# Attention with chunk selection, then an MLP: loads of later batches held behind W2, pair 4 prepared later, some ScalarE work on VectorE, the last rows in two parts

## The chip, the cores and the metric

The kernel runs on one core of one Trainium2 chip. A core has TensorE (matrix products), VectorE, ScalarE, GpSimd and SyncE, each with its own instruction queue that it works off in order, and 16 DMA engines that all queues share. The metric is the device time of one execution in microseconds (us). The time is the median of several runs; the profile is of one execution of its own.

## The reference

There are 4 batches, 8 heads, 768 positions, 64 numbers per head. Keys come in 24 chunks of 32 positions. For each query an upper bound of its scores in each chunk decides which six chunks it may look at. Then come masked attention over these, a layer norm, and an MLP with a residual.

```python
def _attn_ref(q, k, v):
    k_min, k_max = min and max of k over each chunk of 32
    ub = sum over d of maximum(q * k_min, q * k_max)
    ub = where(causal, ub, -1e9)
    top_chunks = argsort(ub)[..., -6:]
    scores = scale * q @ k.T
    scores = where(chunk selected and pos_q >= pos_k, scores, -1e9)
    return softmax(scores) @ v

def _moe_ref(x, g_ln, w_ch1, w_ch2):
    xn = (x - mean(x)) / sqrt(var(x) + 1e-6) * g_ln
    return x + maximum(xn @ w_ch1, 0.0) @ w_ch2
```

x has the 8 heads of a position side by side (512 numbers). W1 is 512 x 2048, W2 is 2048 x 512, all in float32 outside; the kernel works with float16 for the large products.

## The kernel before

**Tiling.** Two heads form a pair, so that 2 x 64 numbers fill 128 partitions. There are 16 pairs, g = 0 to 15, four for each batch; batch 0 has pairs 0 to 3, and pair 4 is the first of batch 1. The 768 positions are six tiles of 128, in two halves (r or i = 0, 1) of three tiles each.

**A pair.** `load_qk` (L190) loads a half of q and k in four transfers on SyncE's queue into tiles of a pool with six buffers per name. `turn` (L219) transposes them on TensorE into PSUM. `q_copy` and `k_copy` bring them to float16: in batch 0 straight into the operands QA, QB, KA, KB on ScalarE; in later batches into `qh` and `kh`, from which SyncE copies them by DMA into QA, QB (`q_ring`) and KA, KB. `k_bound` (VectorE) takes the min and max of each chunk, `k_diag` lays them out (GpSimd for later batches: four small operations), `bounds` (TensorE) forms the upper bounds, `select` (VectorE) finds the six best, `mask_t` and `mask_ring` put the mask into QA and QB as further rows. `scores` are TensorE products followed by an exponential on ScalarE; `diag` (GpSimd) cuts the diagonal; `values` are the products with v, `normalise` and `pair_stats` (VectorE) finish a pair.

**A half of a batch.** When four pairs are done: `stats`, `centre`, `x_t` (transposes on TensorE), `mlp1` (8 groups of 8 matmuls with W1, each group followed by a ReLU on ScalarE, L516), `mlp2` (for each of three tiles 16 matmuls with W2 in four pieces, j = 0 to 3, then on VectorE the scaling and the residual, L530, and the output transfer on SyncE, L535).

**Order.** TensorE is given work of several pairs and of the MLP interleaved. Each call is a piece with a time in units of one pair; the pieces are sorted by it, and the engines work them off in that order. For batch 0 a list (`begin`, with `loads` for the transfers) gives the order and each engine is tied to it; for later pairs `at(t, ...)` gives times relative to T, the time of the pair's first score. `MOVED` holds some 400 small shifts of single pieces.

**Weights.** W1 and W2 are loaded by GpSimd's queue in four pieces each, converted to float16 on the way (`w1_load`, `w2_load`). A one-element copy from `kc`, which some pair's `k_bound` wrote, holds each load back until that pair is so far. V loads go through the same queue. A transfer of GpSimd takes one of eight completion semaphores in turn and waits for the transfer that had it before.

The warm-up matmuls (`warm`, `idle`, L309) write to tiles that nobody reads.

Of the kernel before, what the change touches and what calls it, by code (L numbers as in the profile page):

```python
# [9 lines left out]
ACTF = mybir.ActivationFunctionType  # L10
ALU = mybir.AluOpType
# [8 lines left out]
def kernel(  # L20
# [13 lines left out]
    nc = tc.nc  # L34
# [52 lines left out]
    RT = const.tile([P, S], F16, name="RT", tag="RT")  # L87
    tiny = const.tile([1, 1], F32, name="tiny", tag="tiny")
# [75 lines left out]
    def w2_load(j, g):  # L164
        nc.gpsimd.tensor_copy(w2b[0:1, 4 * j, 0:1], st[g]["kc"][0:1, 0, NCH // 2:NCH // 2 + 1])
        nc.gpsimd.dma_start(w2b[:, 4 * j:4 * j + 4, :], w2_r[:, 4 * j:4 * j + 4, :])

# [22 lines left out]
    def load_qk(g, i):  # L190
        b, hp = divmod(g, HP)
        for nm, src in (("kn", k), ("qn", q)):
            t = st[g][nm, i] = ldp.tile([P, TR, 2, D], F32, name=nm, tag=nm)
            for hh in range(2):
                nc.sync.dma_start(
                    t[:, :, hh], src[b, 2 * hp + hh, i * TR * P:(i + 1) * TR * P].rearrange("(t p) d -> p t d", p=P),
                )

# [72 lines left out]
    def k_copy(g, i):  # L271
        pst = st[g]["kn", i]
        c = cols(g, i)
        if g < HP:
            nc.scalar.copy(KA[g % NK][0:64, c], pst[0:64, :])
            nc.scalar.copy(KB[g % NK][64:P, c], pst[64:P, :])
            return
        kh = smp.tile([P, TR * P], F16, name="kh", tag="kh")
        nc.scalar.copy(kh, pst)  # L279
        nc.sync.dma_start(KA[g % NK][0:64, c], kh[0:64, :])  # L280
        nc.sync.dma_start(KB[g % NK][64:P, c], kh[64:P, :])
# [223 lines left out]
    def mlp1(b, r, m):  # L505
# [10 lines left out]
        nc.scalar.activation(h["hT"][:, m:m + 2], hp_[:, :, 0:TR * P], ACTF.Relu, scale=HS)  # L516

    def mlp2(b, r, i, j):
# [4 lines left out]
        for kt in range(4 * j, 4 * j + 4):  # L523
            nc.tensor.matmul(  # L524
                yp, h["hT"][:, kt, i * P:(i + 1) * P], w2b[:, kt, :],
                start=(kt == 0), stop=(kt == KT2 - 1),
            )
        if j == 3:
            ot = outp.tile([P, DM], F32, name="ot", tag="ot")
            nc.vector.scalar_tensor_tensor(  # L530
                ot, yp, h["rstd"][:, i:i + 1], xh(b, r)[:, i].rearrange("p h d -> p (h d)"),
# [3 lines left out]
            nc.sync.dma_start(out[b, s * P:(s + 1) * P, :], ot)  # L535
# [11 lines left out]
        4: [(load_v, 1, 1), (load_v, 2, 1), (load_qk, 4, 0)],  # L547
        5: [(w2_load, 0, 0), (w2_load, 1, 0), (load_v, 3, 1), (load_qk, 4, 1)],
        6: [(w2_load, 2, 1), (w2_load, 3, 1)],
# [65 lines left out]
    GAP = 0.6  # L615
# [7 lines left out]
    floor = {tuple(args): t for t, _, fn, args, _ in pieces if fn == load_qk}  # L623
    ready = [max(t for t, _, fn, args, _ in pieces if fn == x_t and args[1] == r) + 0.01 for r in range(NR)]
    for g in range(HP, NG):
# [5 lines left out]
        for i in range(2):  # L631
            t = max(T - 1.98 + 0.3 * i, floor.get((g, i), -1.5) + 0.01)
# [5 lines left out]
        at(T - 1.4, q_relu, g)  # L638
        at(T - 1.4, q_ring, g)
        at(T - 1.3, k_diag, g)  # L640
# [21 lines left out]
    for b in range(B):  # L662
# [14 lines left out]
        if b == 0:  # L677
# [13 lines left out]
            (): -0.04, (0, 1): -0.009, (0, 2): -0.025, (1,): 0.008, (1, 1): 0.017, (1, 2): 0.017,  # L691
            (2,): 0, (2, 4): 0.006, (2, 5): 0.028, (3,): 0, (3, 1): 0.013, (3, 2): 0.013,
            (4,): -0.048, (5,): 0.008, (5, 5): 0.016, (6,): 0.004, (7,): -0.067, (7, 1): -0.07,
            (8,): -0.436, (9,): -0.025, (9, 5): -0.02, (11,): -0.044, (12,): -0.311, (13,): -0.144,
            (14,): -0.138, (14, 5): -0.134, (15,): -0.21, (15, 4): -0.176, (15, 5): 0,
        },
        "centre": {
            (): 0.008, (0,): -0.017, (0, 1): 0, (0, 1, 0): -0.017, (1,): 0, (1, 0, 2): 0.089,
            (1, 1): 0.033, (1, 1, 1): 0.026,
        },  # L700
        "diag": {
            (): -0.046, (0, 0): 0.016, (0, 1): 0.001, (1, 0): 0.012, (1, 1): -0.067, (2,): 0.003,
            (3, 0): -0.003, (3, 1): 0, (4,): -0.056, (6, 0): -0.044, (6, 1): -0.066, (7, 0): -0.178,
            (7, 1): -0.097, (8, 0): -0.399, (8, 1): -0.6, (9, 0): -0.066, (9, 1): -0.069, (11, 0): 0,
            (11, 1): -0.054, (12, 0): -0.04, (12, 1): 0, (13, 0): -0.146, (13, 1): -0.078,
            (14, 0): 0.003, (14, 1): 0, (15, 0): -0.621,
        },
        "k_bound": {
            (0,): -0.011, (1,): -0.011, (2,): -0.009, (3,): -0.018, (4, 0): 0.007, (4, 1): 0.027,
            (5, 1): 0.022, (6, 0): 0.002, (6, 1): 0.107, (7,): -0.058, (8, 0): -0.331,  # L710
            (8, 1): -0.396, (9, 0): 0.002, (9, 1): 0.065, (11, 0): -0.008, (11, 1): 0.025,
            (12, 0): -0.017, (12, 1): -0.015, (13,): -0.032, (14,): 0.028,
        },
        "k_copy": {
            (0,): -0.004, (1, 0): 0.161, (1, 1): 0.063, (2,): 0.006, (3, 0): -0.011, (3, 1): 0.054,
            (4,): 0.024, (5, 0): 0.511, (5, 1): 0.42, (6,): 0.038, (7, 0): -0.032, (9, 1): 0.023,
            (10,): 0.034, (11, 1): 0.026, (12, 0): 0.938, (12, 1): 0.253, (13, 0): 0.002,
            (13, 1): 0.073, (14,): 0.046, (15,): 0.034,
        },
        "k_diag": {  # L720
            (1,): 0.041, (2, 0): 0.13, (3, 0): 0.033, (3, 1): 0.01, (4,): -0.002, (6,): 0.002,
            (7,): -0.058, (8,): -0.331, (9,): -0.138, (10,): -0.023, (11,): 0.02, (12,): 0.006,
            (13,): -0.032, (14,): -0.108, (15,): -0.076,
        },
        "load_qk": {
            (): -0.438, (0, 0): 0.085, (0, 1): -0.538, (1, 0): 0.034, (1, 1): -0.331, (2, 0): 0,
            (2, 1): -0.329, (3, 0): 0.16, (3, 1): -0.169, (4, 0): -0.33, (4, 1): -0.667,
            (5, 0): -0.543, (5, 1): -1.259, (6, 0): 0.011, (6, 1): -0.111, (7, 0): 0.064,
            (7, 1): 0.002, (8, 0): -0.299, (8, 1): -0.593, (10, 0): 0.015, (10, 1): -0.002,
            (11, 0): -0.01, (11, 1): -0.012, (12, 0): 0.082, (12, 1): 0.004, (13, 0): 0.11,  # L730
            (13, 1): 0.159, (14,): 0.026, (15, 0): 0.317, (15, 1): 0.334,
        },
        "load_v": {
            (2,): -0.087, (3, 0): -0.13, (3, 1): -0.568, (4,): -0.551, (5,): -0.547, (6,): -0.163,
            (7,): 0.215, (8,): -0.124, (9,): 0.342, (12,): 0.279, (13,): 0.241, (14,): 0.301,
            (15,): 0.238,
        },
        "mask_ring": {
            (): 0.017, (0, 0): 0.021, (0, 1): 0, (1, 0): 0.036, (1, 1): -0.009, (2, 0): 0.023,
            (2, 1): 0, (4,): 0.064, (5,): 0.074, (6,): 0.076, (7,): 0.016, (8,): -0.257, (9,): 0.076,  # L740
            (10,): 0.209, (11,): 0.066, (12,): 0.08, (13,): 0.102, (14,): 0.139, (15,): 0.093,
        },
        "mask_t": {
            (): -0.004, (0,): 0, (1, 0): -0.019, (1, 1): -0.002, (2,): 0.002, (4,): -0.016,
            (5,): -0.068, (7,): -0.064, (8,): -0.337, (10,): -0.001, (11,): -0.014, (12,): 0.002,
            (13,): -0.082, (14,): 0, (15,): -0.006,
        },
        "mlp1": {
            (0, 0, 2): -0.016, (0, 0, 6): 0.106, (0, 0, 10): 0.098, (0, 0, 14): 0.069,
            (0, 1): -0.023, (0, 1, 0): 0, (0, 1, 2): 0.016, (0, 1, 14): 0.055, (1,): -0.026,  # L750
            (1, 0, 0): 0.016, (1, 0, 2): 0.016, (1, 0, 4): 0.028, (1, 0, 8): -0.014,
            (1, 1, 0): -0.036, (1, 1, 4): -0.178, (1, 1, 10): 0, (1, 1, 14): -0.001, (2,): -0.294,
            (2, 0, 6): -0.616, (2, 0, 12): -0.277, (2, 1, 2): -0.353, (2, 1, 6): -0.28,
            (2, 1, 10): -0.228, (3,): 0.103, (3, 0, 2): 0, (3, 0, 4): 0, (3, 0, 12): 0,
            (3, 0, 14): 0, (3, 1, 0): 0, (3, 1, 4): 0.108, (3, 1, 6): 0, (3, 1, 14): 0.094,
        },
        "mlp2": {
            (): -0.156, (0, 0, 1, 0): -0.071, (0, 0, 1, 3): 0, (0, 0, 2, 0): -0.051, (0, 1): -0.154,
            (0, 1, 0): -0.156, (0, 1, 0, 0): -0.184, (0, 1, 0, 3): -0.145, (0, 1, 1, 0): -0.156,
            (0, 1, 1, 1): 0.152, (0, 1, 2, 0): -0.132, (1,): -0.157, (1, 0, 0, 1): 0,  # L760
            (1, 0, 1, 3): -0.053, (1, 1): -0.138, (1, 1, 0): -0.182, (1, 1, 0, 3): -0.138,
            (1, 1, 2, 2): -0.182, (1, 1, 2, 3): -0.182, (2,): -0.298, (2, 0, 0): -0.323,
            (2, 0, 0, 1): -0.46, (2, 0, 0, 3): -0.305, (2, 0, 1, 0): -0.323, (2, 0, 2, 2): -0.34,
            (2, 0, 2, 3): -0.34, (2, 1): 0, (2, 1, 0, 0): -0.34, (2, 1, 0, 1): -0.18,
            (2, 1, 0, 2): -0.323, (2, 1, 0, 3): -0.298, (2, 1, 1, 0): -0.267, (2, 1, 1, 1): -0.298,
            (2, 1, 1, 2): -0.423, (2, 1, 1, 3): -0.568, (3,): -0.233, (3, 0, 0): 0,
            (3, 0, 0, 2): -0.124, (3, 0, 0, 3): -0.233, (3, 0, 2): -0.332, (3, 1, 0, 0): -0.332,
            (3, 1, 0, 1): -0.374, (3, 1, 1, 1): -0.263, (3, 1, 1, 2): -0.443, (3, 1, 1, 3): -0.009,
# [122 lines left out]
```

## Time and profile before

| what | value |
|---|---|
| time, median of 3 runs | 303.1 us (302.56 to 303.96) |
| span of the profiled execution | 301.4 us, TensorE clock 0.997 |
| TensorE busy | 288.2 us (96%) |
| VectorE, ScalarE, GpSimd busy | 190.8, 183.5, 91.1 us |
| DMA traffic | 27.27 MB read from HBM, 6.29 MB written |
| W1 pieces, issue to landing | 6.0, 7.3, 8.2, 10.6 us |
| W2 pieces, issue to landing | 8.1, 10.1, 12.3, 14.3 us |
| mean of one: L524 (mlp2), L512 (mlp1) matmul | 379 ns, 326 ns |
| mean of one: L516 ReLU, L276 K copy on ScalarE | 813 ns, about 470 ns |

The page says PE for TensorE, DVE for VectorE, ACT for ScalarE, POOL for GpSimd, SP for SyncE; a q behind it means that engine's instruction queue. L512 is line 512 of the kernel. Matmuls overlap one another, so that the mean of one is longer than the distance between two, and a TensorE shown as busy may still be working below its best rate.

### The profile page before, as it was taken

The page shows a single profiled execution, that of the slowest core. Times are in us where ns is not written, and L with a number is a line of the kernel's source. Part 1 is how long each engine was busy: PE and PEld are TensorE (multiplying, and loading weights), DVE is VectorE, ACT ScalarE, POOL GpSimd, SP SyncE. Part 2 cuts the span into 40 slices and gives each one's busy share as a digit, 9 for nine tenths or more (in the row PEclk, how much of TensorE's full clock was granted, in tenths as well). Part 3 has the DMA queues.
Part 4 walks back from the last instruction along what each step waited for, and adds up shares of the span by engine and source line. Part 5 has one row for each costly group of instructions (what it writes and reads, how often), then busy time and mean ns, then how long its engine had stood idle before and what let it go on. Part 6 is the DMA issues. An engine that isn't in the chain of part 4 may idle for free.

```text
span 301.4 us, 7194 instructions
## 1 busy us (share of the span) xinstructions
PE 288.2 (96%) x2753; PEld 195.4 (65%) x2753; DVE 190.8 (63%) x654; ACT 183.5 (61%) x274; POOL 91.1 (30%) x162
## 2 busy tenths in 40 slices
PE   7887998999999999999999999999999999999993
PEld 3874766765777676777767667766666555555541
DVE  7888655679998788999577768577262282011011
ACT  3983997664788667778665674848368524423310
POOL 9559383152444412733230411223021120000000
PEclk9999999999999999999999999999999999999998
DMA  7999999999659649679572210113010110010111
GB/s 131 208 210 198 180 199 196 164 193 204 149 135 187 124 72 165 110 143 148 88 132 62 78 46 2 41 49 90 35 37 0 37 37 35 35 37 35 70 37 71
DMA packets 90226, 31.41 MB, mean 104 GB/s; under 512 B 78416, under 2 KB 87120, under 8 KB 90192
## 3 DMA queue, kind: packets, MB, share of 16 engines
q1 hardware_dynamic: 60416, 23.61, 33.8%
q0 software_dynamic: 29248, 7.34, 24.8%
q8 instruction: 22, 0.36, 0.5%
q14 instruction: 12, 0.10, 0.1%
q10 hardware_dynamic: 528, 0.00, 0.1%
HBM read 27.27 MB, written 6.29 MB: 111 GB/s over the span
## 4 chain that ended last, share of the span: by engine, by line
PE 75%; DMA 8%; POOL 7%; issue 4%; DVE 4%; ACT 1%; POOLq 0%; ACTq 0%
PE yp L524 24%; PE mm L512 24%; PE mm L411 10%; PE sm L437 6%; PE tr L223 4%; DMA w2b<-in_moe_w_ch_dram 4%; DMA w1b<-in_moe_w_ch_dram 4%; PE ub L326 3%; POOL va L214 2%; PE trh L497 1%; POOL pt L424 1%; PE trh L354 1%; DVE xc L482 1%; ACT pt L417 1%; POOL rstd L491 1%
## 5 line engine op out<-in xcount | busy, mean ns | idle before, releaser
L417 ACT ACTIVATE pt<-mm 128x1024 f16<-128x1024 f32 (+1 forms) x96 | 86.2, 918 | 25.7 <-PE mm L411 25.3
L524 PE MATMUL yp<-w2b,hT 128*128 128x512 f16 x384 | 95.9, 379 | 1.5 <-DMA w2b<-in_moe_w_ch_dram 1.5
L512 PE MATMUL mm<-xT,w1b 128*128 128x384 f16 x512 | 94.3, 326 | 0.0
L516 ACT ACTIVATE hT<-mm 128x768 f16<-128x768 f32 x64 | 51.9, 813 | 49.1 <-PE mm L512 48.8
L512 PEld LDWEIGHTS <-w1b 128*128 128x128 f16 x512 | 48.9, 98 | 29.9 <-issue 0.2
L524 PEld LDWEIGHTS <-hT 128*128 128x128 f16 x384 | 36.4, 98 | 31.8
L424 POOL TENSOR_SCALAR_AFFINE_SELECT pt<-pt 128x768 f16<-128x768 f16 x32 | 28.8, 899 | 89.1 <-ACT pt L417 89.1
L530 DVE SCALAR_TENSOR_TENSOR ot<-yp,rstd,x 128x512 f32<-128x512 f32 x24 | 17.9, 746 | 45.9 <-PE yp L524 45.9
L411 PE MATMUL mm<-QA,KA 128*128 128x128 f16 (+2 forms) x224 | 34.5, 245 | 1.0 <-ACT hT L516 0.5
L411 PE MATMUL mm<-QB,KB 128*128 128x128 f16 (+2 forms) x224 | 34.2, 246 | 0.0
L437 PEld LDWEIGHTS <-pt 128*128 128x128 f16 x672 | 24.6, 98 | 5.6 <-POOL pt L424 1.8
L437 PE MATMUL sm<-va,pt 128*128 128x65 f16 x672 | 26.5, 193 | 1.4 <-POOL pt L424 1.3
L411 PEld LDWEIGHTS <-KA 128*128 128x128 f16 x224 | 17.9, 99 | 8.1 <-issue 2.3
L471 DVE BATCH_NORM_STATS2 bst<-x 128x6 f32<-128x128 f32 x96 | 21.9, 282 | 0.8
L268 DVE TENSOR_REDUCE kc<-tr 128x12 f32<-128x384 f32 x32 | 17.6, 549 | 6.6 <-PE tr L223 4.9
L411 PEld LDWEIGHTS <-KB 128*128 128x128 f16 x224 | 18.0, 98 | 3.5 <-issue 0.8
L446 DVE RECIPROCAL rden<-sm 128x6 f32<-128x6 f32 x32 | 6.1, 191 | 19.7 <-PE sm L437 19.6
L447 DVE TENSOR_TENSOR x<-sm,rden 128x384 f32<-128x384 f32 x32 | 17.8, 557 | 1.0
L223 PE MATMUL tr<-ident_f,qn 128*128 128x128 f32 x96 | 16.2, 278 | 1.3 <-DMA qn<-in_q_dram 1.3
L269 DVE TENSOR_REDUCE kc<-tr 128x12 f32<-128x384 f32 x32 | 17.5, 547 | 0.0
L279 ACT CAST kh<-tr 128x384 f16<-128x384 f32 x24 | 11.6, 484 | 9.2 <-DMA KB<-kh 3.2
L223 PE MATMUL tr<-ident_f,kn 128*128 128x128 f32 x96 | 16.2, 278 | 0.0
(87 smaller groups left out, 354.2 us busy)
## 6 DMA issues: line engine op xcount, KB each, us to landing
kn<-in_k_dram SPq DMA_DIRECT2D x64, 96.0 KB, 3.3
qn<-in_q_dram SPq DMA_DIRECT2D x64, 96.0 KB, 3.7
out_dram<-ot SPq DMA_DIRECT2D x24, 256.0 KB, 2.1
va<-in_v_dram POOLq DMA_DIRECT2D x12, 192.0 KB, 5.5
w1b<-in_moe_w_ch_dram POOLq DMA_DIRECT2D x4, 512.0 KB, 7.7
w2b<-in_moe_w_ch_dram POOLq DMA_DIRECT2D x4, 512.0 KB, 11.2
KA<-kh SPq DMA_DIRECT2D x24, 48.0 KB, 2.1
KB<-kh SPq DMA_DIRECT2D x24, 48.0 KB, 2.0
```

Of the source, the lines that this page charges most:

```text
L223: nc.tensor.transpose(pst[:, t * P:(t + 1) * P], src[:, t], ident_f)
L268: nc.vector.tensor_reduce(kc[:, 0, n], view, axis=AX.X, op=ALU.min)
L411: nc.tensor.matmul(sc[:, hh, o:o + w * P], ks[:, t * P:(t + 1) * P], qs[:, s * P:(s + w) * P], start=True, stop=True,)
L417: nc.scalar.activation(pt[:, n0:n1].rearrange("p n h x -> p h n x"), sc[:, :, 0:o].rearrange("p h (n x) -> p h n x", x=P), ACTF.Exp, scale ...
L424: nc.gpsimd.affine_select(out=dv, in_=dv, compare_op=ALU.is_ge, fill=0.0, base=0, pattern=[[0, 2 * TR], [1, P]], channel_multiplier=-1,)
L437: nc.tensor.matmul(pv[:, hh, s2, :], pt[:, where[t, s], hh, :], va[:, hh, t, 0:D + 1], start=(t == 0), stop=(t == s),)
L447: nc.vector.tensor_tensor(xh(b, r)[:, :, 2 * hp:2 * hp + 2, :].rearrange("p s h d -> p h s d"), pv[:, :, :, 0:D], rden.to_broadcast([P, 2, ...
L471: nc.vector.bn_stats(h["st"][:, i, hp], xh(b, r)[:, i, 2 * hp:2 * hp + 2].rearrange("p h d -> p (h d)"),)
L512: nc.tensor.matmul(hp_[:, i, 0:TR * P], w1b[:, kt, (m + i) * P:(m + i + 1) * P], h["xT"][:, kt], start=(kt == 0), stop=(kt == KT1 - 1),)
L516: nc.scalar.activation(h["hT"][:, m:m + 2], hp_[:, :, 0:TR * P], ACTF.Relu, scale=HS)
L524: nc.tensor.matmul(yp, h["hT"][:, kt, i * P:(i + 1) * P], w2b[:, kt, :], start=(kt == 0), stop=(kt == KT2 - 1),)
L530: nc.vector.scalar_tensor_tensor(ot, yp, h["rstd"][:, i:i + 1], xh(b, r)[:, i].rearrange("p h d -> p (h d)"), op0=ALU.mult, op1=ALU.add,)
```

## The change

**q/k loads held.** Before the first load of pair 4, SyncE issues a tiny transfer (`fence`) that reads one element of W2's last piece, so it has to wait until that piece is there; all later q/k loads are ordered after it. Meant: W1 and W2 have the DMA engines to themselves. **W2 earlier in the list.** W2's pieces wait for pair 3's `kc`, go out in pairs, and V's second halves are spread between the weights; pair 4's loads move from list entries 4 and 5 to 6. **Pair 4 later.** Its transposes and copies get the time -1.0 (`LATE`), where before they followed their load. **ScalarE's work on VectorE.** In the first MLP half (b, r) = (0, 0), every second ReLU (m = 2, 6, 10, 14) is a `tensor_scalar` on VectorE; in batch 0 the second-half copy into KB is too. **The last tile** of the last half is computed in two column parts, 384 and then 128 columns, with eight of the 16 row blocks per call, and each part is scaled and written out by itself. **MOVED** is redone throughout.

```diff
     def w2_load(j, g):
-        nc.gpsimd.tensor_copy(w2b[0:1, 4 * j, 0:1], st[g]["kc"][0:1, 0, NCH // 2:NCH // 2 + 1])
+        nc.gpsimd.tensor_copy(w2b[0:1, 4 * j, 0:1], st[g]["kc"][0:1, 0, 0:1])
...
     def load_qk(g, i):
         b, hp = divmod(g, HP)
+        done = nc.cur_bb.bb.instructions
+        if (g, i) == (HP, 0):
+            nc.sync.dma_start(fence, w2b[0:1, KT2 - 1, 0:1])
+            held.append(done[-1].name)
+        n = len(done)
...
+        if held:
+            for one in done[n:]:
+                if one.engine == nc.sync.engine:
+                    tc.add_manual_dep(one, held[0], order, reason="order")
...
-            nc.scalar.copy(KB[g % NK][64:P, c], pst[64:P, :])
+            (nc.scalar.copy if i == 0 else nc.vector.tensor_copy)(KB[g % NK][64:P, c], pst[64:P, :])
...
-        nc.scalar.activation(h["hT"][:, m:m + 2], hp_[:, :, 0:TR * P], ACTF.Relu, scale=HS)
+        if (b, r) == (0, 0) and m % 4 == 2:
+            nc.vector.tensor_scalar(
+                h["hT"][:, m:m + 2], hp_[:, :, 0:TR * P], 0.0, HS, op0=ALU.max, op1=ALU.mult,
+            )
+        else:
+            nc.scalar.activation(h["hT"][:, m:m + 2], hp_[:, :, 0:TR * P], ACTF.Relu, scale=HS)
...
-        for kt in range(4 * j, 4 * j + 4):
+
+        n, cs = 4, slice(0, DM)
+        if (b, r, i) == (B - 1, NR - 1, TR - 1):
+            n, cs = 8, slice(0, DM - P) if j < 2 else slice(DM - P, DM)
+        for kt in range(n * j % KT2, n * j % KT2 + n):
             nc.tensor.matmul(
-                yp, h["hT"][:, kt, i * P:(i + 1) * P], w2b[:, kt, :],
+                yp[:, cs], h["hT"][:, kt, i * P:(i + 1) * P], w2b[:, kt, cs],
                 start=(kt == 0), stop=(kt == KT2 - 1),
             )
-        if j == 3:
+        if kt == KT2 - 1:
...
-        4: [(load_v, 1, 1), (load_v, 2, 1), (load_qk, 4, 0)],
-        5: [(w2_load, 0, 0), (w2_load, 1, 0), (load_v, 3, 1), (load_qk, 4, 1)],
-        6: [(w2_load, 2, 1), (w2_load, 3, 1)],
+        4: [(load_v, 1, 1), (w2_load, 0, 3), (w2_load, 1, 3)],
+        5: [(load_v, 2, 1), (w2_load, 2, 3), (w2_load, 3, 3), (load_v, 3, 1)],
+        6: [(load_qk, 4, 0), (load_qk, 4, 1)],
...
-    GAP = 0.6
+    GAP, LATE = 0.6, -1.0
...
-            t = max(T - 1.98 + 0.3 * i, floor.get((g, i), -1.5) + 0.01)
+            t = max(T - 1.98 + 0.3 * i, LATE + 0.25 * i if g == HP else -9.0)
...
-        at(T - 1.4, q_relu, g)
-        at(T - 1.4, q_ring, g)
-        at(T - 1.3, k_diag, g)
+        t = max(T - 1.4, t + 0.1)
+        at(t, q_relu, g)
+        at(t, q_ring, g)
+        at(t + 0.1, k_diag, g)
```

## The prediction, made before the changed kernel ran

> **What bounds the kernel now.** I read the page's busy shares and slices first, then the table of windows, then TensorE's timeline, then the landing times of single transfers. The page:
>
> ```profile
> PE 288.2 (96%) x2753; PEld 195.4 (65%) x2753; DVE 190.8 (63%) x654; ACT 183.5 (61%) x274; POOL 91.1 (30%) x162
> ...
> PE   7887998999999999999999999999999999999993
> ...
> DMA  7999999999659649679572210113010110010111
> ```
>
> TensorE is the bound, but not evenly: apart from the last slice only the first seven (to 53 us) fall below 9, and there the DMA engines are full (they stay so to about 75 us). The table of windows (columns: busy us and count of PE, PEld, DVE, ACT, POOL; clock; DMA share; GB/s) shows who sets the pace there:
>
> ```profile
> 20.00:24.00 4.00, 2.55 (x49) 2.03 (x50) 3.26 (x13) 2.53 (x4) 2.74 (x5) 1.00 1.23 228
> ...
> 32.00:36.00 4.00, 4.00 (x34) 3.22 (x33) 2.34 (x11) 3.93 (x9) 0.76 (x1) 1.00 1.41 173
> 36.00:40.00 4.00, 3.66 (x28) 2.65 (x26) 2.01 (x11) 3.94 (x8) 3.36 (x6) 1.00 1.69 182
> 40.00:44.00 4.00, 3.60 (x33) 2.67 (x33) 2.07 (x5) 4.00 (x7) 3.41 (x8) 1.00 1.26 205
> 44.00:48.00 4.00, 4.00 (x40) 3.38 (x39) 2.67 (x5) 3.93 (x9) 1.61 (x3) 1.00 1.24 200
> 48.00:52.00 4.00, 3.42 (x47) 2.27 (x44) 2.70 (x13) 3.21 (x5) 2.02 (x3) 1.00 1.20 192
> 52.00:56.00 4.00, 3.04 (x25) 2.26 (x25) 2.40 (x7) 1.85 (x3) 0.00 (x0) 1.00 1.39 177
> ```
>
> From 29 to 49 us ScalarE has no idle time while VectorE is little over half busy: TensorE is paced by ScalarE's evictions. Busy TensorE hides this, so I count its work: a W1 matmul costs 0.1625 us in a dense run (8 in 1.30), a W2 matmul 0.216 (4 in 0.86), a 128x128 one 0.055, an f32 transpose 0.107. From mlp1's start at 28.4 to mlp2's first matmul at 49.5 the queue holds 17.5 us of such work: 3.6 us are lost. From 80 us on some 1 us in 10 is lost, so 28 to 53 is where something can be won. Then W2 itself is late:
>
> ```profile
> 49.53 1.89 PE L524 MATMUL yp<-w2b,hT 128*128 128x512 f16 x8
> 52.96 0.38 PE L524 MATMUL yp<-w2b,hT 128*128 128x512 f16 x1 [1.54 <-DMA w2b<-in_moe_w_ch_dram]
> ```
>
> The reason stands in GpSimd's timeline: two V loads wait for W1 pieces to land, and W2's issue stands behind them.
>
> ```profile
> 32.34 0.76 POOL L214 DMA_DIRECT2D va<-in_v_dram  x1 [1.82 <-DMA w1b<-in_moe_w_ch_dram]
> 36.02 0.77 POOL L214 DMA_DIRECT2D va<-in_v_dram  x1 [2.93 <-DMA w1b<-in_moe_w_ch_dram]
> ```
>
> W2's four pieces are issued at 38.15 to 41.88 and land 8.1, 10.1, 12.3 and 14.3 us later (46.3 to 56.2). SyncE is meanwhile loading q/k of batch 1 (its first load issues at 19.5).
>
> **What the Trainium skill says.** DMA: Bandwidth & Descriptors, section Issuing engines are not separate DMA queues: transfers from all engines interleave on the same 16 DMA engines. The trace agrees: a kn load lands in 4.2 to 6.0 us at 14 to 18 us, and in 13.8 to 14.1 when issued at 42 to 46 among W2. VectorE: DVE Perf Modes, section Why PSUM operands drop a tier: an fp32 operand in PSUM is read one element a cycle; here 384 such elements take 0.549 us (the k reduce) and 512 take 0.746 (the output eviction). PSUM — Partial Sum Buffer, section PSUM bank collisions raise a hardware error: a bank must not be touched by two engines at once, even in different columns, so it has to be guarded as a whole; no run here shows a collision.
>
> **The change part by part.**
>
> *ScalarE's relief.* Four ReLUs leave ScalarE (0.70 us each in its dense run, 2.8) and four K copies (0.48, 1.9); pair 4's two q/k evictions that stand at 47.7 and 48.8 (0.39 + 0.5) move past the stretch. Of 20.2 us of dense ScalarE work from 29.1, 15.3 remain, ending near 44.5.
>
> *VectorE's load.* It takes four ReLUs of 128x768 from PSUM. No row shows this; I extend 384 → 0.549 and 512 → 0.746: at least 0.80 (768 at 0.96 GHz, page above), at most 1.1; I take 0.87. The copies take about 0.4: 5.1 us in all. Summing the changed program's VectorE queue from the first xT copy (28.1) to the masks before mlp2 gives 17.1 us: it fits, ending near 46, but with hardly any slack.
>
> *TensorE.* Its total work is unchanged (the same matmuls, the same fillers). From 28.2 the changed order holds 16.7 us before mlp2's first matmul; with about 1 us in 10 lost (buffer rotation behind the four exponentials of pair 0), it gets there at 46.3 instead of 49.5.
>
> *W2 earlier.* In the new GpSimd order two W2 pieces go out right after rstd (0,0), with no landing to wait for; only the second two follow a V load that waits for W1's last piece. From 24 us no q/k loads compete. A W piece alone: they follow each other at 3.3 to 3.4 us (49.55, 52.92, 56.2) with some q/k beside, at 4.8 to 5.2 with q/k in full flow (22.1, 27.3, 32.1); a V or q/k transfer takes some 0.4 us of the engines. Taking off the q/k share leaves 2.3 to 2.9 per piece. W1 then lands at 22, 25, 30.5, 33; W2 at 36, 39, 43 and 45.4 to 48. mlp2's ninth matmul needs the third piece at about 48: no wait, and 1.5 us come free. At that matmul the changed kernel leads by 53.0 - 48.0 = 5.0 us.
>
> *The fence, a new wait.* SyncE waits for W2's last piece (call it F, 45.4 to 48, I take 46.7). Behind it on SyncE stand 28 q/k transfers of batch 1 (0.52 us each, the start of the trace), then pair 4's K and Q ring copies and the first output. TensorE's turn of pair 4's q comes 3 us of work after mlp2's ninth matmul, at 51.1. q lands at F + 0.5 (fence) + 4 x 0.52 + about 2.7 = F + 5.3 = 52: a stall of 0.9 (0 to 2.2). The Q ring copy issues at about F + 17.4 = 64 and lands 2 to 5 us later; pair 4's first score is due at 67.5: 0 to 1.5, I take 0.3. The bounds of pair 4 need k_bound, then four GpSimd operations (1.3 us): about 0.3. Lead left: 5.0 - 1.5 = 3.5; VectorE is as full as before at 68 to 76, where centring holds x_t (0.2 more). So 3.3.
>
> *Later pairs.* Everything from 80 us on is re-placed by fractions of a microsecond around a TensorE that is busy 30.0 of 30 us: 0, give or take 1.
>
> *The last rows.* Before:
>
> ```profile
> 288.04 8.80 PE L524 MATMUL yp<-w2b,hT 128*128 128x512 f16 x40
> ...
> 296.88 0.75 DVE L530 SCALAR_TENSOR_TENSOR ot<-yp,rstd,x 128x512 f32<-128x512 f32 x1 [2.70 <-PE yp L524]
> ```
>
> From the last tile's first matmul to the end of its eviction: 16 x 0.216 + 0.04 + 0.75 = 4.25. In the changed program the first matmul of the 128-column part waits for the eviction of the 384-column part (same bank). So: 16 x 0.1625 = 2.60, eviction 0.60, handover 0.1, 16 x 0.055 = 0.88 and 0.1 to drain, eviction of 128 columns 0.30 (128x256 takes 0.417, 128x384 0.548): 4.58. That is 0.3 later; the last transfer is 64 KB instead of 256 and may win 0.1 (before 2.1 us to landing). I take +0.3; without that wait it would be -0.5.
>
> Sum: -3.3 + 0.3 + 0 = -3.0, so 303.1 - 3.0 = 300.1.
>
> **The rivals.**
> - *Batch 1's q/k come late (15%).* If W pieces still take 3.3 us, F is 49.5, pair 4's q stalls TensorE 3.7 us instead of 0.9, the ring copies follow as late: lead 3.3 - 2.8 = 0.5, and 303.1 - 0.5 + 0.3 = 302.9. For: SyncE is in order, and everything on it waits behind one transfer. Against: the window before W2's landing is then free of q/k.
> - *VectorE becomes the bound (10%).* With ReLUs at 1.1 and masks queued behind them the stretch ends 1.5 us later: 301.7. For: 17.1 of some 18 us filled. Against: ReLUs are interleaved, every second one stays on ScalarE.
> - *More is won (17%).* No stalls (1.5) and the re-placed later pairs give 0.5: 298.2. For: ScalarE links at 85, 119 and 167 us in the chain of waits. Against: TensorE shows no idle there.
> - *Slower (10%).* F at 52 and ring copies at 0.7 us a transfer: q at 57.3 is 6.2 late against a lead of 5.0, the Q ring then lands another 2 us after its score: 303.1 + 1.2 + 2 + 0.3 = 306.6. For: in before, transfers issued at 42 to 54 went out at only 4 in 8 us. Against: that was contention with W2, which the fence removes.
>
> **How the numbers follow.** My forecast, 300.1, has 48%. The limit of "faster" is 301.6: nearly all of the forecast, the 17% above it, half of the VectorE case and a little of the late case make 70%; the rest of these, 19%, is within 0.5%; slower 11%. The range 298.0 to 303.5 takes in the late and VectorE cases and half of the better one; the slower case and the other half stay out.
>
> **What would show it.** W2's wait before the ninth mlp2 matmul gone; mlp2's first matmul at 46 to 47.5; ScalarE with idle time between 30 and 48, VectorE near full; W2's last piece landed by 48 and the fence then; a wait of 0 to 2 us on q at TensorE near 51; the last 128-column matmuls waiting for VectorE about 0.7 us. I am wrong if mlp2 still starts after 48.5, if TensorE stands over 3 us on q, k or a ring copy between 50 and 70, or if the lead at 80 us is under 2 or is lost afterwards.

## The result, and the profile after

| | before | changed |
|---|---|---|
| median of four runs | 302.8 us (302.4 to 304.0) | 306.6 us (305.8 to 307.0) |
| ratio to before, 95% interval | | 1.0115 [1.008, 1.0149] |
| span of the profiled execution | 301.4 us | 304.3 us |

The changed kernel is slower by 1.2%, where 1% faster was predicted. The profiled executions are 2.9 us apart, the medians 3.7; what is read from the two traces below adds up to the 2.9. A few executions of each kernel take 2 to 3 us longer than the rest, most of them at a mean clock of 0.98 to 0.99; the ratios count them, the medians hardly do. The page shows little of it: TensorE is as busy as before, ScalarE has less to do and VectorE more.

```profile
PE 289.1 (95%) x2769; PEld 197.0 (65%) x2769; DVE 194.7 (64%) x663; ACT 178.9 (59%) x266; POOL 93.1 (31%) x162
...
PE   7888999998979999999999999999999999999994
...
DMA  7999999999569579397590210112000001000011
```

New are two slices below 9 after the weights' phase (the tenth, 68 to 76 us, and the twelfth, 84 to 91; before, both were 9). The windows (columns as in the prediction) show the stretch that was to be relieved, and two later ones:

```profile
28.00:48.00 20.00, 19.65 (x185) 15.24 (x183) 14.92 (x46) 15.72 (x30) 11.79 (x21) 1.00 1.44 184
...
68.00:72.00 4.00, 3.16 (x45) 2.13 (x44) 3.03 (x8) 1.96 (x4) 1.07 (x2) 1.00 0.89 199
...
80.00:84.00 4.00, 3.06 (x37) 2.43 (x36) 2.24 (x13) 1.46 (x3) 0.39 (x1) 1.00 0.44 99
```

Before, it was this from 28 to 48:

```profile
28.00:48.00 20.00, 19.13 (x160) 14.52 (x158) 12.64 (x40) 19.30 (x37) 11.64 (x20) 1.00 1.36 191
```

ScalarE was busy 19.30 of the 20 us and VectorE 12.64: that relief came as meant (15.72, 14.92). But TensorE is idle 0.84 and 0.94 us in two later windows in which it was full before (4.00 in both). TensorE's timeline says where. The lines below are four places of it; a bracket is the idle time ahead of the line and what ended it.

```profile
48.07 2.11 PE L548 MATMUL yp<-w2b,hT 128*128 128x512 f16 x9
...
64.49 0.24 PE L341 MATMUL ub<-BH,q 128*128 128x96 f16 x2 [0.46 <-POOL BH L313]
...
71.69 0.22 PE L426 MATMUL mm<-QA,KA 128*128 128x128 f16 x1 [0.74 <-DMA QA<-q]
...
85.56 0.38 PE L426 MATMUL mm<-QA,KA 128*128 128x256 f16 x2 [2.50 <-ACT pt L432]
```

The same two places in before, pair 4's bounds and the scores of the last line:

```profile
64.75 0.25 PE L326 MATMUL ub<-BH,q 128*128 128x96 f16 x2
...
82.77 0.38 PE L411 MATMUL mm<-QA,KA 128*128 128x256 f16 x2
```

Read against before, these are four states of the lead. mlp2's nine matmuls run in one piece at 48.07, before it was at 49.53 and the ninth waited for W2: a lead of 1.5 us, and 3.2 at the ninth matmul (48.07 + 8 x 0.216 = 49.8, before 53.0), of which 0.7 is no gain: two transposes of pair 4 (0.33 to 0.36 each) that before stand ahead of mlp2 now stand behind it. So 2.5. At pair 4's bounds (64.49, before 64.75) 0.3 is left. At pair 4's first scores it is gone. The last line is a stall that nothing in the prediction led to; the values matmuls just ahead of it stand at 82.54 (before 82.40, 0.14 behind), the scores after it at 85.56 (before 82.77, 2.8 behind), and at 91.4 us the lag is 3.0.

What is lost between 49.8 and 64.5 us is not one wait. The brackets show two (0.19 on `q`, 0.46 on BH), but they leave out idle time that the modelled ends of matmuls cover. Counted from one start to the next, less what the matmuls in between cost when they run densely, TensorE stands 2.15 us from mlp2's ninth matmul to pair 4's bounds, and 0.06 in before. The 2.15 are 0.26 for q of pair 4 to land, 0.36 for VectorE's copy of that q, 0.62 for BH, 0.67 in three waits for ScalarE's exponentials, and 0.25 for VectorE's copy of pair 3's mask into QB.

The line at 85.56 names ScalarE's exponential (`pt`), but that had not been slow. ScalarE's timeline shows what it stood behind, and SyncE's when that was issued:

```profile
84.11 0.48 ACT L294 CAST kh<-tr 128x384 f16<-128x384 f32 x1 [2.65 <-DMA KB<-kh]
```

```profile
46.93 0.73 SPq L199 DMA_DIRECT2D fence<-w2b  x1
...
80.42 0.59 SPq L296 DMA_DIRECT2D KB<-kh  x1
```

`kh` is a copy of K with two buffers; a third copy has to wait until the DMA from it into KB has landed. That DMA stands in SyncE's queue, which the fence held until 46.93 and which then issues loads, outputs and ring copies without a pause until 108 us. So the copy into `kh` waits for a transfer issued at 80.42 and landed 3.6 us later, the exponential waits behind it on ScalarE, and TensorE waits for the exponential. From there to the last rows the lag grows only from 3.0 to 3.2 us.

The tail: the second column part waits for the eviction of the first, as expected. From the end of the last eviction to the end of the program it takes 2.9 us, in before 3.75.

```profile
299.89 1.05 PE L548 MATMUL yp<-w2b,hT 128*128 128x128 f16 x16 [0.71 <-DVE ot L554]
```

### The profile page after: what moved, and what is told of

Read it like the earlier page. It is cut to its first block, busy times and chain, and to the rows that moved or that the text cites. A ratio compares the mean times of both kernels' runs of the same rounds, so it can differ in the third digit from the quotient of the medians.

```text
span 304.3 us, 7241 instructions
## 1 busy us (share of the span) xinstructions
PE 289.1 (95%) x2769; PEld 197.0 (65%) x2769; DVE 194.7 (64%) x663; ACT 178.9 (59%) x266; POOL 93.1 (31%) x162
## 4 chain that ended last, share of the span: by engine, by line
PE 73%; DVE 10%; POOL 6%; ACT 3%; issue 3%; DMA 3%; SPq 1%; POOLq 0%; ACTq 0%
PE yp L548 25%; PE mm L527 24%; PE mm L426 9%; PE sm L452 5%; PE tr L238 4%; PE ub L341 3%; ACT pt L432 2%; POOL va L229 2%; PE ub L331 2%; DMA QA<-q 1%; PE trh L512 1%; DVE bst L486 1%; DMA KB<-kh 1%; POOL pt L439 1%; DVE xc L497 1%
## 5 line engine op out<-in xcount | busy, mean ns | idle before, releaser
L432 ACT ACTIVATE pt<-mm 128x1024 f16<-128x1024 f32 (+2 forms) x96 | 86.2, 920 | 28.2 <-PE mm L426 27.9
L548 PE MATMUL yp<-w2b,hT 128*128 128x512 f16 (+2 forms) x400 | 95.6, 370 | 0.8 <-DVE ot L554 0.7
L536 ACT ACTIVATE hT<-mm 128x768 f16<-128x768 f32 x60 | 48.7, 812 | 46.1 <-PE mm L527 43.9
L548 PEld LDWEIGHTS <-hT 128*128 128x128 f16 x400 | 37.2, 98 | 32.8 <-issue 1.9
L554 DVE SCALAR_TENSOR_TENSOR ot<-yp,rstd,x 128x512 f32<-128x512 f32 (+2 forms) x25 | 18.2, 726 | 54.5 <-PE yp L548 50.9
L283 DVE TENSOR_REDUCE kc<-tr 128x12 f32<-128x384 f32 x32 | 17.5, 546 | 4.1 <-ACT kh L294 2.3
L516 ACT ACTIVATE xT<-trh,gstr 128x384 f16<-128x384 f16 x16 | 9.1, 580 | 13.4 <-PE trh L512 13.4
L238 PE MATMUL tr<-ident_f,kn 128*128 128x128 f32 x96 | 16.4, 279 | 0.3 <-DVE q L262 0.2
```

Source lines behind the costliest of these rows:

```text
L238: nc.tensor.transpose(pst[:, t * P:(t + 1) * P], src[:, t], ident_f)
L283: nc.vector.tensor_reduce(kc[:, 0, n], view, axis=AX.X, op=ALU.min)
L432: nc.scalar.activation(pt[:, n0:n1].rearrange("p n h x -> p h n x"), sc[:, :, 0:o].rearrange("p h (n x) -> p h n x", x=P), ACTF.Exp, scale ...
L548: nc.tensor.matmul(yp[:, cs], h["hT"][:, kt, i * P:(i + 1) * P], w2b[:, kt, cs], start=(kt == 0), stop=(kt == KT2 - 1),)
L554: nc.vector.scalar_tensor_tensor(ot[:, cs], yp[:, cs], h["rstd"][:, i:i + 1], xh(b, r)[:, i].rearrange("p h d -> p (h d)")[:, cs], op0=ALU ...
```

## The experiments

Each ratio is to runs of the kernel before on the same chip (medians of before 302.8 to 303.2 us). Where "bounds" are given, it is the time of pair 4's first bounds matmul in the trace (64.75 before, 64.49 changed). Single traces differ by up to 0.9 us already at the first values matmul of pair 0 (16.0 to 16.9 us; in run 10 it stands at 18.8, so its 68.23 is some 2.4 us late from the start), so small shifts are read as distances inside a trace.

| edit | median, us | ratio [95%] | bounds |
|---|---|---|---|
| changed kernel | 306.57 | 1.0115 [1.008, 1.0149] | 64.49 |
| 1 without the fence | 307.67 | 1.0136 [1.0076, 1.0196] | 68.49 |
| 2 four `kh` buffers | 304.03 | 1.0026 [1.0008, 1.0044] | 64.89 |
| 3 last tile whole | 306.52 | 1.0102 [1.0069, 1.0135] | |
| 4 ReLUs and K copies on ScalarE | 306.28 | 1.0094 [1.0055, 1.0133] | |
| 5 before, with VectorE's part | 302.72 | 0.9986 [0.9962, 1.001] | |
| 6 before, four `kh` buffers | 303.37 | 1.0018 [0.9997, 1.0039] | |
| 7 = 2 with before's later order | 303.17 | 1.0011 [0.9992, 1.0031] | 64.64 |
| 8 = 2 with ring copies on GpSimd | 306.51 | 1.0111 [1.0089, 1.0132] | 65.81 |
| 9 = 7, fence on W2's third piece | 302.79 | 0.9979 [0.9963, 0.9996] | 64.17 |
| 10 = 9, pair 4 placed at 50 us | 305.37 | 1.0073 [1.0044, 1.0102] | 68.23 |
| 11 = 7 with two `kh` buffers | 305.23 | 1.0067 [1.0042, 1.0091] | 64.18 |
| 12 = 7, ReLUs and copies on ScalarE | 303.91 | 1.0027 [1.0011, 1.0044] | 65.42 |
| 13 = 7, pair 4's loads ahead of W2 | 303.07 | 0.999 [0.997, 1.001] | 64.63 |
| 14 = 13, pair 4 placed at 50 us | 302.90 | 0.9965 [0.9946, 0.9984] | 64.51 |
| 15 = 13, pair 4 placed at 47 us | 302.90 | 0.9974 [0.9952, 0.9996] | 64.16 |
| 16 = 14, pair 3's mask first | 301.76 | 0.9956 [0.9939, 0.9973] | 63.19 |
| 14 again, beside 16 again | 302.62 | 0.998 [0.9966, 0.9993] | 64.22 |
| 16 again | 301.75 | 0.9943 [0.9923, 0.9963] | (see below) |

### First: the changed kernel with one part undone (1 to 4)

**1, without the fence** (the fence and `held` lines of `load_qk` left out):

> The changed kernel without the fence; all else as changed. Theory A (SyncE's queue, held until 46.9 us, has to issue 28 loads, the ring copies and the first outputs without a pause until about 82 us; late ring copies stall ScalarE on kh and TensorE behind it): the stall at 82.5 to 85.6 us (2.5 us on TensorE) and the wait on QA at 71 us (0.7) go; W2's last piece lands later than 46.9, at 50 to 53, and costs 0 to 1.5 us before mlp2. Time 301.5 to 304, at least 2.5 below the changed kernel. Rival B (the late preparation of pair 4 and VectorE's load lose the time, whatever SyncE does): 305.5 to 307.

**2, four `kh` buffers:**

```diff
-        kh = smp.tile([P, TR * P], F16, name="kh", tag="kh")
+        kh = smp.tile([P, TR * P], F16, name="kh", tag="kh", bufs=4)
```

> The changed kernel with four buffers for kh instead of two. Theory A: ScalarE no longer waits for a K ring copy's landing at 81.5 to 84.1 us, so the TensorE stall of 2.5 us goes, and most of it stays gained: 303.5 to 305. Rival C (SyncE's backlog is met again at the next place, scores waiting for KA, KB or QA themselves): at most 0.7 us gained, 305.8 to 306.6.

**3, last tile whole** (the line `n, cs = 8, ...` and its condition left out):

> The changed kernel with the last tile computed and written in one part. By the two traces, the last eviction ends 0.5 us later with two parts, but from there to the end it takes 2.97 us instead of 3.77: undone, the time goes up by 0.3 us (306.9). The prediction said that two parts cost 0.3 us: then 306.3.

**4, scalar back** (`if (b, r) == (0, 0) and m % 4 == 2` becomes `if False`; KB's copies on ScalarE again):

> The changed kernel with the four ReLUs and the four K copies back on ScalarE. If their move to VectorE was worth what the prediction said (ScalarE paces TensorE between 29 and 49 us), mlp2 starts 1.5 to 3 us later than 48.1; what of it is left at the end depends on SyncE: the backlog is fixed by the fence at 46.9, so theory A says that little of it counts: 306.5 to 308. Rival B (VectorE's extra load costs time): 304 to 306.

Run 1 came out above both ranges. As theory A said, without the fence the `kh` stall and the wait on QA are gone, but W2 is late and costs more than the 1.5 us allowed for. TensorE's timeline, then the windows of that run:

```profile
48.38 1.89 PE L545 MATMUL yp<-w2b,hT 128*128 128x512 f16 x8
52.49 0.58 PE L545 MATMUL yp<-w2b,hT 128*128 128x512 f16 x1 [2.22 <-DMA w2b<-in_moe_w_ch_dram]
```

```profile
52.00:54.00 2.00, 1.51 (x8) 0.93 (x8) 0.56 (x2) 0.00 (x0) 0.00 (x0) 0.58 1.25 192
54.00:56.00 2.00, 2.00 (x8) 0.98 (x7) 0.15 (x1) 1.02 (x1) 0.00 (x0) 0.56 1.54 160
```

The wait of 2.22 us is followed by 4 us at a clock of 0.57 (the third column from the end): the run is 4.0 us behind the changed kernel from 54 us on. The Trainium skill (TensorE: Matmul & The Clock Gate, section What's actually happening) has it that an idle window of about 3.4 us halves the clock, and that the window runs freely. This trace agrees with the halving, but not with the length: TensorE was idle for about 2.4 us (the eight matmuls from 48.38 cost 0.216 each, the ninth starts at 52.49). The 2.50 us stall of the changed kernel left its clock at 1.00. So in these traces the fence is worth about 4 us at 54 us, and what stands behind it takes about 3 back. One of run 1's four executions took 306.9 us at a mean clock of 1.00; where that one lost its time was not traced.

The second thing in run 1: from pair 4's q transposes to its bounds it takes 57.89 to 68.49, 10.60 us, and in the changed kernel 53.89 to 64.49, 10.60 too. The loads were there long before in run 1, so their delay does not cause what is lost there.

Run 2 confirmed the buffers: the 2.50 us stall is gone and the time is 2.5 us shorter (306.57 to 304.03). Run 3 can't be told from the changed kernel by time, and in the traces neither: from the eviction of the row tile before the last to the end of the program it takes 7.66 us with the last tile whole and 7.65 in two parts (7.95 in before). Run 4 can't be told from it either: mlp2 begins at 49.11, 1.0 us later (1.5 to 3 were expected), and nothing of that is left at the end.

### Single parts in before, and what the later order costs (5 to 8)

**5, VectorE's part alone in before** (the ReLU and KB lines of the change): 

> The kernel before with only the VectorE part of the change: four ReLUs of the first half and the K copies of the second sub-tile (pairs 0 to 3) on VectorE. Theory D (TensorE loses only about 1.6 us from 28 to 49 us in the kernel before, and what ScalarE gives up there is eaten again before the first pair of the second batch has its bounds): mlp2 starts about 0.5 to 1 us sooner than 49.5, the time is 302.3 to 303.3, within 0.3% of before. Rival (as the prediction counted, 3.6 us are lost there and come back): 299.5 to 300.5.

**6, four buffers in before:**

> The kernel before with four kh buffers instead of two, the control of the run with four in the changed kernel. Theory A (the two buffers hurt only where SyncE issues the ring copies late, behind the fence and the queued loads): before does not wait there on TensorE, so 302.6 to 303.1. Rival (two buffers cost in any order): 301.5 or less.

**7, the later order put back** (2, and the old table for every piece but loads in pairs 5 and later and in MLP halves after the first; the last tile's `mlp2` keeps the new shifts):

```diff
-        one, key = MOVED.get(fn.__name__, {}), tuple(...)
+        late = key[:2] >= (0, 1) if fn.__name__ in BYHALF else key[:1] >= (5,)
+        one = (OLD if late else MOVED).get(fn.__name__, {})
```

> The changed kernel with four kh buffers, and with the shifts of the kernel before for all that is not a load in pairs 5 and later and in all MLP halves after the first. Theory E (the rest of the loss after 86 us comes from the new order of the later pairs): about 0.5 to 1.6 us faster than the changed kernel with four buffers alone, 302.4 to 303.5. Rival (the later order is neutral, and the rest is carried from the first 86 us): 304.0, plus or minus 0.4.

**8, ring copies on GpSimd** (2, with `ring = nc.gpsimd if g < HP + 3 else nc.sync` issuing the copies into QA, QB, KA, KB):

> The changed kernel with four kh buffers, and with the ring copies of pairs 4, 5 and 6 issued by GpSimd's queue instead of SyncE's, where loads stand ahead of them. Theory A2 (SyncE's backlog behind the fence costs the 0.7 to 1.2 us wait on QA as well): that wait goes, 302.8 to 303.4. Rival (GpSimd stands in the chain that prepares pair 4's bounds, and its issues delay BD and BH): the wait goes but the bounds come later, 304 or more.

5: mlp2 begins at 49.18 instead of 49.53 (0.5 to 1 us sooner was expected) and then waits 2.11 us for W2: the help alone meets the next wait. The trace is of an execution of 305.1 us, where the median is 302.7; its clock fell after that wait. 6: two buffers cost nothing in the old order. 8: the rival was right. Six issues of 0.5 to 0.6 us stand around BD and BH on GpSimd, the wait on BH is 1.74 us instead of 0.46 and the bounds come at 65.81.

7 is 0.9 us below 2 by median, but 0.5 by the ratios, whose intervals overlap. The spans differ by 1.7 us (300.9 against 302.6), of which 0.75 is that run 2's trace is of an execution of 304.8 us, above its median. So that the new later order costs time is likely, not shown. TensorE's timeline of run 2 and of run 7 shows one reason:

```profile
72.55 0.22 PE L426 MATMUL mm<-QA,KA 128*128 128x128 f16 x1 [1.19 <-DMA QA<-q]
72.61 2.97 PE L548 MATMUL yp<-w2b,hT 128*128 128x512 f16 x13
```

```profile
70.82 2.75 PE L548 MATMUL yp<-w2b,hT 128*128 128x512 f16 x12
...
74.53 0.22 PE L426 MATMUL mm<-QA,KA 128*128 128x128 f16 x1
```

In the new order pair 4's first score stands ahead of the 13 mlp2 matmuls, and waits 1.19 us for the copy into QA. In the old one it stands behind them and the copy, issued no sooner (68.36 against 68.10), is there.

### Where the lead of 48 us goes (9 to 12)

**9, the fence on W2's third piece** (in 7, `w2b[0:1, KT2 - 5, 0:1]`):

> As the run with the later order put back and four kh buffers (303.2, span 300.9), with the fence reading W2's third piece instead of its last: SyncE's loads start some 2 to 3 us sooner. Theory F (pair 4's place in the order, not the loads, costs what is lost from 54 to 64.5 us): the 0.48 us wait on q goes, the wait on BH before pair 4's bounds stays at 0.3 to 0.5, time 302.7 to 303.3. Rival (the loads are what is late): the bounds come 1.5 us or more sooner, 301.7 or less.

**10, and pair 4 sooner** (`LATE = -1.15`):

> The same, with pair 4's preparation also placed sooner (its q transposes right after the ninth mlp2 matmul, about 50 us, instead of at 54). Theory F: with 4 us more between preparation and bounds the wait on BH is gone and the lead over before at pair 4's bounds grows from 0.1 to 1 to 2 us: 301.5 to 302.4. Rival (that stretch is limited by VectorE and ScalarE whatever the place): within 0.3 of the run without it. If the loads aren't there at 50 us, TensorE waits on q instead and it ends at 303 or above.

**11, two buffers with the later order put back:**

> The changed kernel with the later order of before, and its own two kh buffers. Theory A (two buffers and SyncE's backlog make the stall, whatever the order): TensorE stands 1.5 to 2.6 us behind the exponential at 82 to 86, 304.5 to 306. Rival (the new later order brings K copies closer together and so makes the stall): no such stall, 303.2 plus or minus 0.4.

**12, 7 with the work back on ScalarE:**

> The later order put back, four kh buffers, and the ReLUs and K copies back on ScalarE. Theory D (VectorE's help brings nothing in the end, because pair 4's chain eats the lead): 302.9 to 303.5, no more than 0.3 from the same kernel with them on VectorE. Rival (with the later stalls gone the help of VectorE counts): 0.7 to 1.5 slower, 304 or more.

11 confirms that two buffers and the backlog make a stall in the old later order too (1.86 us on `kh`, then 1.77 on TensorE; 305.23 against 303.17). 12 fell between the expected bands (302.9 to 303.5, and 304 or more): with the later stalls gone, VectorE's help counts 0.74 us by the medians (303.91 against 303.17), but the ratios' intervals overlap. 9 agrees with theory F: the loads start 2 us sooner, q's wait is gone, BH's wait stays at 0.46. 10 was no test of it: q was not there at 50 us and TensorE waited for it.

```profile
54.33 0.52 PE L238 MATMUL tr<-ident_f,qn 128*128 128x128 f32 x3 [1.62 <-DMA qn<-in_q_dram]
```

### Place, or VectorE's order (13 to 16)

**13, pair 4's eight loads ahead of W2** (7 with the fence at pair 5, and the two `load_qk` of pair 4 in entries 4 and 5 of `loads`):

> The later order put back, four kh buffers, and pair 4's eight q/k loads issued before W2 as in the kernel before; the fence then holds only pairs 5 and later. Pair 4 keeps its place in the order of the changed kernel. Theory F (the place in the order costs the stretch from 54 to 64.5 us): no wait on q, but the 0.46 us wait on BH stays, pair 4's bounds at 63.9 to 64.6, 302.5 to 303.3. Rival (loads): bounds at 63 or sooner, under 302. If eight loads ahead of W2 make its third piece late, a wait on W2 of 1 us or more stands before the ninth mlp2 matmul, and it ends above 304.

**14 and 15, pair 4 sooner** (13 with `LATE = -1.15`, and with `-1.3`):

> The same, with pair 4's preparation placed right after the ninth mlp2 matmul (about 50 us). Theory F: q is there, so no wait; BH is ready long before the bounds, the wait of 0.46 goes, bounds at 62.5 to 63.5, end 0.7 to 1.5 us sooner than without the earlier place: 301.4 to 302.4. Rival (VectorE and ScalarE limit that stretch whatever the place): within 0.3 us of the run without it.

> The same, with the first half of pair 4's preparation placed ahead of mlp2's first matmul (about 47 us), nearest to the kernel before. Theory F: as the run at 50, 301.2 to 302.4. Rival (work put before mlp2 delays mlp2 by what it takes, 1 us, and only moves it): mlp2 at 49, bounds and end within 0.3 of the run that keeps pair 4 late.

Theory F's forecast fell, and the rival's, within 0.3 us, came. With its data there and its place at 54, 50 or 47 us, pair 4's bounds come at 64.63, 64.51 and 64.16; from mlp2's first matmul that is 16.2, 16.0 and 15.3 us, the last with two transposes (0.7) already done ahead of mlp2. At 54 us the waits are those of the changed kernel without q's (1.90 us by the same count). At 50 us pair 4's own waits go, BH's among them, but another takes their place, here in TensorE's timeline of run 14, and in VectorE's:

```profile
60.77 0.34 PE L369 MATMUL trh<-ident_h,MN 128*128 128x128 f16 x3 [1.37 <-DVE MN L360]
```

```profile
57.77 0.32 DVE L269 TENSOR_SCALAR r<-q 128x640 f16<-128x640 f16 x1
58.00 0.82 DVE L270 SCALAR_TENSOR_TENSOR r<-q 128x640 f16<-128x640 f16 x1
58.73 0.55 DVE L283 TENSOR_REDUCE kc<-tr 128x12 f32<-128x384 f32 x1
59.20 0.55 DVE L284 TENSOR_REDUCE kc<-tr 128x12 f32<-128x384 f32 x1
59.66 0.18 DVE L359 MAX8 m<-ub 128x8 f32<-128x24 f32 x1
59.76 0.73 DVE L554 SCALAR_TENSOR_TENSOR ot<-yp,rstd,x 128x512 f32<-128x512 f32 x1
60.41 0.30 DVE L360 TENSOR_TENSOR MN<-ub,m 128x144 f16<-128x144 f32 x1
```

MN is pair 3's last mask. Its sixth MAX8 and the comparison stand behind pair 4's ReLU terms, its two K reduces, and an output eviction. Moved up in VectorE's order, by three shifts:

**16, the mask first:**

```diff
+    MOVED["select"] = {**MOVED.get("select", {}), (3, 1): -0.15}
+    MOVED["q_relu"] = {**MOVED.get("q_relu", {}), (4,): 0.25}
+    MOVED["q_ring"] = {**MOVED.get("q_ring", {}), (4,): 0.25}
```

> As the run with pair 4's loads first and its preparation at 50 us, with pair 3's last mask placed ahead of pair 4's ReLU terms and last K reduces on VectorE. Theory G (the lead is held up by VectorE's order: the mask that TensorE waits 1.37 us for stands behind pair 4's operations): that wait falls under 0.4, pair 4's bounds come at 63.2 to 63.8 instead of 64.4, 301.7 to 302.5. Rival (VectorE has no room for it in any order, since it holds 12.7 us of work in these 16.5 and each of its results is waited for): the wait moves to BH or to another mask, bounds at 64.2 or later, 302.6 to 303.2.

VectorE's timeline of run 16 at the same place:

```profile
54.59 0.63 DVE L359 MAX8 m<-ub 128x8 f32<-128x24 f32 x6
55.25 0.31 DVE L360 TENSOR_TENSOR MN<-ub,m 128x144 f16<-128x144 f32 x1
...
57.36 0.32 DVE L269 TENSOR_SCALAR r<-q 128x640 f16<-128x640 f16 x1
57.59 0.82 DVE L270 SCALAR_TENSOR_TENSOR r<-q 128x640 f16<-128x640 f16 x1
```

The mask is done about 5 us sooner, TensorE's longest wait in brackets from 48 us to the bounds is 0.2 (0.96 us in all by the count above, 1.84 in run 14), and from mlp2's first matmul to the bounds it takes 15.1 us, where run 14 took 16.0 and the changed kernel 16.4. Since part of the difference between the two traces was there before mlp2, both were run once more beside each other:

> The kernel with pair 4's loads first and its preparation at 50 us once more, beside the next one and in as many rounds. Theory G: 302.6 to 303.1, the wait on pair 3's mask 1.2 to 1.5 us. Rival: as the next one, within 0.3 us.

> The kernel with pair 3's last mask ahead of pair 4's work on VectorE once more. Theory G: 0.7 to 1.3 us faster than the run beside it, no wait on the mask over 0.4 us. Rival (the earlier difference came from the start of the execution, 0.4 us of it at mlp2's first matmul, and from scatter): within 0.3 us of it.

302.62 and 301.75, with intervals that don't meet; from mlp2 to bounds 16.0 and 15.1 us again (the trace of run 16 again began 3.6 us late, after a clock of 0.50 to 0.65 from 12 to 20 us, so its own times stand apart). With pair 4 at 50 us it is VectorE's order that costs, not the amount of its work: it does 13.0 us of work in the 16.5 us from 48 in run 16 and 12.7 in run 14. (On TensorE two mlp2 matmuls moved behind the mask's transposes with it.) Place and order are both needed; the order with pair 4 left at 54 us was not run, and there TensorE waited for the mask's copy for no more than 0.25 us. Run 16 is also the fastest of all: 0.9943 [0.9923, 0.9963] of before, by the medians 301.75 against 303.17.

## Why the prediction was wrong

- **ScalarE's relief, VectorE's load: right in size, worth less.** ScalarE 15.7 us instead of 19.3 from 28 to 48. (The 15.3 left of 20.2 takes off three ReLUs, not the four named; the fourth stands at 55.6 in before, outside the stretch.) The ReLU on VectorE took 0.96 (0.87 taken), the copy 0.56 (0.4); VectorE was idle 5 of the 20 us, more than "hardly any slack". At mlp2's start the relief is worth about 1.0 us (run 4).
- **TensorE's work ahead of mlp2: a term mis-sized.** "17.5 us of such work: 3.6 us are lost" counted six f32 bounds matmuls a half at 0.107 each. The trace has two records for each, and the chain of waits shows `31.80 1.32 PE ub L331 x12`: 1.3 us a half instead of 0.65. Three halves lie in the stretch, so 2 us more work and only 1.6 lost in before. mlp2 came at 48.07, not 46.3.
- **W2 and F, its last landing: right.** The last piece landed at 46.9 (46.7 taken), no wait on W2.
- **"Leads by 53.0 - 48.0 = 5.0": half of it.** 1.8 was the term above, and 0.7 was work that the new order only puts behind the mark. 2.5 remained.
- **"Lead left: 5.0 - 1.5 = 3.5": waits left out.** Only waits for pair 4's own data were taken off. Up to the bounds these came to 1.24 us (q 0.26, its copy 0.36, BH 0.62; taken were 0.9 for q and 0.3 for BH). That q cost so little was luck: it landed at 53.75 instead of 52, and TensorE, late by the term above and a fourth half of bounds, came for it at 53.6 instead of 51.1. Another 0.92, on the exponentials and the mask's copy, was not counted at all. So 2.2 us of the lead went by 64.5. Why these engines are later there than in before was not tested in the changed kernel itself; runs 14 to 16 show VectorE's order as the cause only for pair 4 placed at 50 us. After the bounds the Q ring cost 0.74 (0.3 taken; it issued at 67.3 instead of 64).
- **What stood behind the fence: put at nothing, the largest loss.** "then pair 4's K and Q ring copies" was followed to the first copies and no further. The queue had no pause until 108 us, and at 80 a ring copy held a buffer of two that ScalarE needed: 2.5 us at once (runs 2 and 11). Before's own page had that wait (3.2 us on `kh` at 74.5), with no harm then to TensorE.
- **Later pairs "0, give or take 1": at the edge of it.** With four buffers the new order costs 0.9 us by the medians and 0.5 by the ratios (run 7 against 2), and neither is clear of the scatter. In run 2's trace pair 4's first score ahead of 13 matmuls waits 1.2; the rest was not traced.
- **Last rows: the wait right, the gain not there.** The wait was 0.71 as thought, and the shorter last transfer won 0.5 instead of 0.1 against run 3 (2.9 us from the last eviction to the end instead of 3.5). The two cancel: two parts came out even with one, where +0.3 was taken.

Sum of the two traces: 2.5 won, 2.2 lost up to the bounds, 0.4 at the Q ring, 2.7 at `kh`, 0.4 in the rest, 0.3 won in the tail (which run 3 has too): 2.9 slower, as the spans. With the buffers and the later order undone (run 7) the kernel is as fast as before. The slower rival's 306.6 was near, but its road (F at 52, slow ring copies) was not taken: F was on time.

## What to carry to other kernels

A fence on an in-order queue moves everything behind it, so follow that queue until it has drained, and for each transfer in it ask which buffer it releases and who fills that buffer next; a pool of two that a DMA empties is as much a wait as the data itself. A lead at a mark is worth what it is only if both orders have done the same work there, and part of it goes wherever another engine has newer work ahead of the older work that TensorE needs next, as VectorE had in run 14. When undoing parts singly shows nothing (here VectorE's help: nothing in the changed kernel, perhaps 0.7 us once the stalls behind it were gone), undo the later stalls first.

## What the runs showed of the hardware

- A wait of 2.1 to 2.2 us on W2 was followed by about 4 us at a clock of 0.5 to 0.7 in the traces of runs 1 and 5. A stall of 2.5 us at 83 us in the changed kernel was not, nor were waits of 1.5 us on W2 in before and of 1.8 us in run 11.
- An f32 bounds matmul of 128x48 gives two records and takes 0.22 us, an f32 transpose of 128x128 takes 0.11.
- From the end of the last eviction to the end of the program it took 2.9 to 3.2 us with a last output of 64 KB, and 3.5 to 3.75 with one of 256 KB (before and runs 3, 5 and 6).
